# Attention outputs per query tile, and weight column sums at another place of the program

## The chip, the cores and the metric

The kernel runs on one core of a Trainium2 chip. The metric is the time of one execution on the device, in microseconds (us). A core has a matrix engine (PE, with its weight loads shown apart as PEld), a vector engine (DVE), an activation engine (ACT) and a general engine (POOL). SP issues the transfers. Each engine has a queue and executes it in order; the engines wait for one another through semaphores.

## The reference

The output of windowed attention goes through two feed-forward layers.

```
scores = q k^T / 8 - slope_h * (i - j)     for 0 <= i - j < 128, else masked
x  = softmax(scores) v                     4 batches, 8 heads of 64, 576 positions
h  = relu(x w_in1);   x2 = (s * h*h + b) w_out1      2304 tokens, 512 -> 2048 -> 512
h2 = relu(x2 w_in2);  out = (h2*h2) w_out2           512 -> 2048 -> 512
```

All values are float32.

## The kernel before

Tokens are handled in blocks of 256: two for each batch (b, u with u = 0 or 1), and one last block, the tail, of the 64 left-over positions of the four batches. The products of the feed-forward layers take each operand as a high and a low part (names ending in h and l) and make three products of them, so that 12 matmuls make one 128-row slice of the hidden layer (L338, names h) and 12 use it again (L374 in the first layer, L383 in the second, names o).

**Jobs.** One job is a call of `mlp` for one block: for each of 16 slices f, `first(f)` is 12 matmuls, a relu on ACT (L342, names r), a square on DVE (L343), and a split into high and low part (names g: a copy on ACT, L95, and a subtraction on DVE, L98, or on POOL, L101). The products with w_out of a slice follow two slices later. The jobs of the first layer are: the first halves of blocks 0 and 1 (a0, a1, 8 slices each), their other halves (c0, c1), then a2 to a6 one after the other in a loop, then a7 together with the tail, a8, which runs six slices behind it. The second layer has b0 with b1, then b2 to b6, b8, b7. `POOL_STEPS` says how many of every four slices of a job have their subtraction on POOL.

**Weights.** They arrive as 64-bit words and are converted in five operations (`convert`: ACT L120, DVE L121, ACT L122, DVE L123, POOL L124; names st), then split (names wih, wil, woh, wol with the number of the group of four slices). The weights of the first layer are converted during a0 to c0, those of the second during a7, a8 and b0.

**Attention.** `pair_unit` handles two heads (hp) of a block. `probabilities` makes the scores (L235) of two query tiles of 128, the exponentials and their sums. `outputs` scales the probabilities, transposes them in pieces of 128 x 128 (L256) into a PSUM bank t, copies the bank to pt, and multiplies by V (L265) into a bank u, where head 0 stands in the partitions 0 to 63 and head 1 in 64 to 127. A query tile has two key blocks, but the first tile of u = 0 has one. These units are hung behind the slices of the jobs before them.

**Column sums.** The b of the first layer reaches the second through the sums of w_out1 over its rows. `sum_rows` adds the high and low rows of a slice to `csum` on POOL (L488, 32 additions in all), `sum_column` adds over the partitions on PE (L511, names pc) and makes `bcol`; `load_y(i)` loads the sums of block i (xib, for blocks 0 and 1 in two parts with xjb, added at L498), scales them and adds bcol (L500, ACT), and splits them (yb0h, yb0l, ...). All of this stands in a7 and a8, as `pieces` spread over 0.9 of their steps, but `load_y(1)`, which stands behind them.

The order of each engine's queue is not that of the program: a scheduler rearranges it when the kernel is built.

Of the kernel before, what the change touches and what calls it, by code (L numbers as in the profile page):

```python
# [8 lines left out]
F32 = mybir.dt.float32  # L9
# [6 lines left out]
P = 128  # L16
# [3 lines left out]
def attention_mlp2_kernel(ctx, tc, first0, first1, qkv0, qkv1, qkvt, w_in1, w_out1, s_in, b_in, w_in2, w_out2, out):  # L20
# [20 lines left out]
    NRAW, NQKV, NPR, NPT = 3, 3, 4, 2  # L41
# [24 lines left out]
                            pattern=[[1, 2 * W]], channel_multiplier=-1)  # L66
    ones = const.tile([P, 1], F32, tag="ones", name="ones")
# [26 lines left out]
    def act_copy(o, i):  # L94
        nc.scalar.activation(o, i, AF.Copy)  # L95
# [100 lines left out]
    def pair_unit(b, u, hp):  # L196
# [48 lines left out]
        def outputs():  # L245
            raw, den, probs, pts = (made[x] for x in ("raw", "den", "probs", "pts"))
            vr = raw[:, BLK + nj * P:n].rearrange("p (j a d) -> p j a d" if early else "p (a j d) -> p j a d", j=nj, d=D)
            for a in range(2):
                tp = (psum("h", f"t{nm}").rearrange("p (i n) -> p i n", n=P) if early and not (a or u) else
                      ps.tile([P, 4, P], F32, tag="t", name=f"t{nm}{a}", bufs=1))  # L250
                m = 0
                for i, (_, ncol) in enumerate(tiles):
                    pr = probs[a][:, i, :ncol]
                    nc.vector.tensor_scalar(pr, pr, den[:, 2 * a + i:2 * a + i + 1], None, ALU.mult)
                    for j in range(ncol // P):
                        nc.tensor.transpose(tp[:, m, :], pr[:, j * P:(j + 1) * P], ident)  # L256
                        m += 1
                (nc.vector.tensor_copy if early and u <= a else act_copy)(pts[a][:, :m, :], tp[:, :m, :])
            up = ps.tile([P, 3 * P], F32, tag="u", name=f"u{nm}", bufs=1) if hp % 2 or u or not early else psum("o", f"u{nm}")

            steps = [(slice(0, 2), 0), (slice(2, 3), P)] if u == 0 else [(slice(0, 1), 0), (slice(1, 3), 0), (slice(3, 4), P)]
            steps = sorted(zip(range(nj), steps), key=lambda x: x[1][0].start - x[1][0].stop)
            for k, (j, (sl, col)) in enumerate(steps):
                for a in range(2):
                    nc.tensor.matmul(up[a * D:(a + 1) * D, col:col + (sl.stop - sl.start) * P], vr[:, j, a, :], pts[a][:, sl, :],  # L265
                                     start=(k == 0), stop=(k == nj - 1), skip_group_check=True)
            xh, xl = xt[(b, u)]
            split(xh[:, hp, :], xl[:, hp, :], up[:, :BLK], act_copy if early and u else act_mark, dve_sub)
# [143 lines left out]
    POOL_STEPS = {"a0": 4, "c1": 3, "a2": 2, "a3": 3, "a5": 3}  # L412
# [58 lines left out]
    nc.sync.dma_start(b_sb, b_in.partition_broadcast(P))  # L471
    tails = [[lambda b=b, hp=hp: tail_unit(b, hp) for hp in range(H // 2)] for b in range(B)]
    for i in range(NHALF, LAST - 1):
        more = attn(i + 2) if i + 2 < LAST and blocks[i + 2] not in xt else []
        pending += tails[i - 3] if i > 2 else []
        mlp([(f"a{i}", xt.pop(blocks[i]), finish1(f"a{i}", acc_dram[i]))], wts1, second_t, FS, pending + more[:5])
        pending = more[5:]

# [5 lines left out]

    def sum_rows(g, j):

        for w in (wts1[g][2], wts1[g][3]):
            nc.gpsimd.tensor_tensor(csum, csum, w[:, j, :].bitcast(F32), ALU.add)  # L488
# [16 lines left out]
    csum = bp.tile([P, DM], F32, tag="csum", name="csum", bufs=1)  # L505
    nc.gpsimd.memset(csum, 0.0)

# [12 lines left out]
    pieces = [lambda g=g, j=j: sum_rows(g, j) for g in range(NG) for j in range(GF)] + [lambda: None] * 6  # L520
    pieces += [sum_column, lambda: ys.update({0: load_y(0)})]
# [63 lines left out]
```

## Time and profile before

| | |
|---|---|
| median of 3 runs | 1028.07 us (1027.82 to 1029.13) |
| profiled execution | 1028.07 us, of which the span of the profile is 1026.3 us |
| mean granted TensorE clock | 0.985 of full speed |
| PE busy | 97% |
| DVE, ACT, POOL busy | 53%, 46%, 17% |

The span is what the profiler saw of the program; 1.8 us lie outside of it. A busy share is a mean over stages that have different limits.

### The profile page before, as it was taken

To read this page: it belongs to the slowest core of one execution; us is meant where nothing else is said; L and a number is where in the kernel's file an instruction comes from. 1 tells how busy PE (TensorE), PEld (TensorE's weight loads), DVE (VectorE), ACT (ScalarE), POOL (GpSimd) and SP (SyncE) were. 2 spreads that over 40 slices of the span, in tenths; PEclk is the share of its full clock that TensorE was granted. 3 is DMA by queue.
4 is the path that set the end of the run, shared out by engine and by line. 5 is a ranking of instruction groups with operands and counts; after the bars stand their busy time and mean duration, and the time that the engine had idled before them with its cause. 6 is when DMAs were issued, how large, how long until landed. Compare 5 with 4: busy or idle time off the path is not lost.

```text
span 1026.3 us, 17924 instructions
## 1 busy us (share of the span) xinstructions
PE 995.3 (97%) x7048; PEld 893.3 (87%) x7048; DVE 540.7 (53%) x1283; ACT 476.1 (46%) x1178; POOL 179.3 (17%) x156
## 2 busy tenths in 40 slices
PE   7898999999999999999899989999999999999998
PEld 4586898889889889899799979989998999999897
DVE  6989864343444534534687788775333333323232
ACT  6676554554544545544324576674232323323232
POOL 4655411001110001100694212210000000000000
PEclk9799999999999999999999999999999999999999
DMA  7264342111121211210402244422010000000000
GB/s 286 83 216 139 103 119 62 47 38 37 52 74 34 70 48 52 67 45 25 159 27 82 83 145 144 147 100 83 2 42 1 22 21 1 21 1 21 1 21 21
DMA packets 39556, 70.36 MB, mean 69 GB/s; under 512 B 4016, under 2 KB 16304, under 8 KB 39472
## 3 DMA queue, kind: packets, MB, share of 16 engines
q1 hardware_dynamic: 39472, 69.22, 20.5%
q8 instruction: 55, 0.90, 0.4%
q14 instruction: 29, 0.24, 0.1%
HBM read 58.72 MB, written 10.49 MB: 67 GB/s over the span
## 4 chain that ended last, share of the span: by engine, by line
PE 81%; DVE 11%; ACT 3%; issue 2%; DMA 2%; SPq 0%; DVEq 0%; ACTq 0%
PE ob L383 17%; PE hb L338 17%; PE ha L338 17%; PE oa L374 15%; PE u L265 4%; PE s L235 3%; DVE st L121 2%; PE hc L338 2%; PE oc L374 2%; PE t L256 2%; DVE gb L98 1%; DVE ra L343 1%; DVE ga L98 1%; DVE rb L343 1%; DVE wol L98 1%
## 5 line engine op out<-in xcount | busy, mean ns | idle before, releaser
L374 PE MATMUL oa<-ga,woh 128*128 128x256 f32 x1024 | 198.2, 288 | 8.7 <-DVE ga L98 8.1
L383 PE MATMUL ob<-woh,gb 128*128 128x512 f32 x576 | 198.5, 392 | 0.9 <-DVE gb L98 0.9
L374 PEld LDWEIGHTS oa<-ga,woh 128*128 128x128 f32 x1024 | 161.8, 192 | 14.1 <-DVE ga L98 9.2
L374 PE MATMUL oa<-ga,wol 128*128 128x256 f32 x512 | 146.2, 287 | 1.2 <-DVE wol L98 1.2
L343 DVE TENSOR_TENSOR rb<-rb 128x256 f32<-128x256 f32 x144 | 64.3, 447 | 120.3 <-ACT rb L342 117.2
L383 PEld LDWEIGHTS ob<-woh,gb 128*128 128x128 f32 x576 | 108.5, 189 | 21.0 <-DVE gb L98 1.3
L343 DVE TENSOR_TENSOR ra<-ra 128x256 f32<-128x256 f32 x128 | 76.5, 602 | 89.2 <-ACT ra L342 88.5
L342 ACT ACTIVATE rb<-hb 128x256 f32<-128x256 f32 x144 | 55.0, 383 | 136.9 <-PE hb L338 126.7
L383 PE MATMUL ob<-wol,gb 128*128 128x512 f32 x288 | 113.5, 394 | 0.0
L374 PEld LDWEIGHTS oa<-ga,wol 128*128 128x128 f32 x512 | 98.6, 193 | 3.9 <-issue 2.3
L98 DVE TENSOR_TENSOR gb<-rb,gb 128x256 fp32r<-128x256 f32 x144 | 68.6, 479 | 61.3 <-ACT gb L95 36.8
L124 POOL TENSOR_TENSOR st<-st 128x1024 int32<-128x1024 int32 (+1 forms) x34 | 65.7, 1932 | 155.0 <-DVE st L123 134.7
L95 ACT ACTIVATE gb<-rb 128x256 fp32r<-128x256 f32 x144 | 60.0, 417 | 67.4 <-DVE rb L343 67.4
L95 ACT ACTIVATE ga<-ra 128x256 fp32r<-128x256 f32 x128 | 52.8, 415 | 69.7 <-DVE ra L343 69.0
L342 ACT ACTIVATE ra<-ha 128x256 f32<-128x256 f32 x128 | 47.9, 378 | 68.5 <-PE ha L338 62.3
L101 POOL TENSOR_TENSOR ga<-ra,ga 128x256 fp32r<-128x256 f32 x40 | 32.7, 822 | 222.3 <-ACT ga L95 185.4
L98 DVE TENSOR_TENSOR ga<-ra,ga 128x256 fp32r<-128x256 f32 x88 | 54.4, 622 | 27.7 <-ACT ga L95 27.3
L383 PEld LDWEIGHTS ob<-wol,gb 128*128 128x128 f32 x288 | 54.6, 189 | 6.8
L188 ACT ACTIVATE pr<-pr,nd 128x128 f32<-128x128 f32 (+1 forms) x96 | 45.1, 472 | 21.8 <-DVE nd L184 21.8
L121 DVE SCALAR_TENSOR_TENSOR st<-st 128x1024 int32<-128x1024 int32 (+1 forms) x34 | 48.2, 1419 | 11.4 <-ACT st L120 11.4
L122 ACT ACTIVATE st<-st 128x1024 f32<-128x1024 f32 (+1 forms) x34 | 37.5, 1108 | 22.8 <-DVE st L121 22.6
L235 PE MATMUL s<-raw 64*128 64x256 f32 (+1 forms) x224 | 43.1, 401 | 4.0 <-DVE nd L184 2.5
(258 smaller groups left out, 2537.8 us busy)
## 6 DMA issues: line engine op xcount, KB each, us to landing
st<-w_in SPq DMA_DIRECT2D x16, 1024.0 KB, 5.7
st<-w_out SPq DMA_DIRECT2D x14, 1024.0 KB, 4.9
raw<-qkv SPq DMA_DIRECT2D x36, 128.0 KB, 2.8
xib<-acc SPq DMA_DIRECT2D x9, 512.0 KB, 3.4
out<-obb SPq DMA_DIRECT2D x16, 256.0 KB, 2.1
raw<-qkv SPq DMA_DIRECT2D x24, 160.0 KB, 3.0
acc<-xoa SPq DMA_DIRECT2D x14, 256.0 KB, 2.0
raw<-qkv SPq DMA_DIRECT2D x12, 192.0 KB, 2.9
```

The lines of the kernel that those rows point to most:

```text
L95: nc.scalar.activation(o, i, AF.Copy)
L98: nc.vector.tensor_tensor(o, a, b_, ALU.subtract)
L121: nc.vector.scalar_tensor_tensor(l32, h32, -2 ** 31, l32, ALU.bitwise_and, ALU.bitwise_or)
L124: nc.gpsimd.tensor_tensor(l32, h32, l32, ALU.add)
L188: nc.scalar.activation(pr, pr, AF.Exp, bias=nmx, scale=-1.0, accum_out=den)
L235: nc.tensor.matmul(sps[a][:, i, :ncol], qr[rows, i * P:(i + 1) * P], kr[rows, ka:ka + ncol], start=(i == 0), stop=True, skip_group_check=True)
L265: nc.tensor.matmul(up[a * D:(a + 1) * D, col:col + (sl.stop - sl.start) * P], vr[:, j, a, :], pts[a][:, sl, :], start=(k == 0), stop=(k == ...
L338: nc.tensor.matmul(ph, w_[:, cc, j * P:(j + 1) * P], x_[:, cc, :], start=(k == 0), stop=(k == 3 * NCC - 1))
L342: nc.scalar.activation(r, ph, AF.Relu)
L343: nc.vector.tensor_tensor(r, r, r, ALU.mult)
L374: nc.tensor.matmul(po[o // 2][:, (o % 2) * BLK:(o % 2 + 1) * BLK], w_[:, j, o * P:(o + 1) * P], g[:, gi, :], start=(start and n == 0 and o ...
L383: nc.tensor.matmul(po[t], g[:, gi, t * P:(t + 1) * P], w_[:, j, :], start=(start and n == 0), stop=(stop and n == 2))
```

## The change

The diff does three things. In `outputs`, a bank t and its copy pt now hold both heads of one query tile (before: both tiles of one head). The products with V are all of 128 columns, and go through the tiles and key blocks with head 0 and head 1 in turn; `tc.issue_after(moved.ins)` is put around them. The column sums become pieces of the jobs a2 to a5 (four slices in each), `csum` is taken from the pool of constants, NRAW (buffers for finished blocks) goes from 3 to 2, and a2, a3 and a5 have no subtraction on POOL any more. The pieces of a7 and a8 are now `sum_column` and `load_y(0)` alone.

```diff
-    NRAW, NQKV, NPR, NPT = 3, 3, 4, 2
+    NRAW, NQKV, NPR, NPT = 2, 3, 4, 2
...
+    csum = const.tile([P, DM], F32, tag="csum", name="csum")
...
-            for a in range(2):
-                tp = (psum("h", f"t{nm}").rearrange("p (i n) -> p i n", n=P) if early and not (a or u) else
-                      ps.tile([P, 4, P], F32, tag="t", name=f"t{nm}{a}", bufs=1))
+            for i, (_, ncol) in enumerate(tiles):
+                tp = (psum("h", f"t{nm}").rearrange("p (i n) -> p i n", n=P) if early and not (i or u) else
+                      ps.tile([P, 4, P], F32, tag="t", name=f"t{nm}{i}", bufs=1))
                 m = 0
-                for i, (_, ncol) in enumerate(tiles):
+                for a in range(2):
                     pr = probs[a][:, i, :ncol]
                     nc.vector.tensor_scalar(pr, pr, den[:, 2 * a + i:2 * a + i + 1], None, ALU.mult)
                     for j in range(ncol // P):
                         nc.tensor.transpose(tp[:, m, :], pr[:, j * P:(j + 1) * P], ident)
                         m += 1
-                (nc.vector.tensor_copy if early and u <= a else act_copy)(pts[a][:, :m, :], tp[:, :m, :])
+                moved = (nc.vector.tensor_copy if early and u <= i else act_copy)(pts[i][:, :m, :], tp[:, :m, :])
             up = ps.tile([P, 3 * P], F32, tag="u", name=f"u{nm}", bufs=1) if hp % 2 or u or not early else psum("o", f"u{nm}")
 
-            steps = [(slice(0, 2), 0), (slice(2, 3), P)] if u == 0 else [(slice(0, 1), 0), (slice(1, 3), 0), (slice(3, 4), P)]
-            steps = sorted(zip(range(nj), steps), key=lambda x: x[1][0].start - x[1][0].stop)
-            for k, (j, (sl, col)) in enumerate(steps):
-                for a in range(2):
-                    nc.tensor.matmul(up[a * D:(a + 1) * D, col:col + (sl.stop - sl.start) * P], vr[:, j, a, :], pts[a][:, sl, :],
-                                     start=(k == 0), stop=(k == nj - 1), skip_group_check=True)
+            with tc.issue_after(moved.ins):
+                k = 0
+                for i, (ka, ncol) in enumerate(tiles):
+                    nk = ncol // P
+                    for j in range(nk):
+                        for a in range(2):
+                            nc.tensor.matmul(up[a * D:(a + 1) * D, i * P:(i + 1) * P], vr[:, ka // P + j, a, :],
+                                             pts[i][:, a * nk + j, :], start=(k == 0), stop=(j == nk - 1),
+                                             skip_group_check=True)
+                        k += 1
...
-    POOL_STEPS = {"a0": 4, "c1": 3, "a2": 2, "a3": 3, "a5": 3}
+    POOL_STEPS = {"a0": 4, "c1": 3}
...
+    def sum_rows(g, j):
+
+        for w in (wts1[g][2], wts1[g][3]):
+            nc.gpsimd.tensor_tensor(csum, csum, w[:, j, :].bitcast(F32), ALU.add)
+
+    nc.gpsimd.memset(csum, 0.0)
+    sums = [lambda g=g, j=j: sum_rows(g, j) for g in range(NG) for j in range(GF)]
     tails = [[lambda b=b, hp=hp: tail_unit(b, hp) for hp in range(H // 2)] for b in range(B)]
     for i in range(NHALF, LAST - 1):
         more = attn(i + 2) if i + 2 < LAST and blocks[i + 2] not in xt else []
         pending += tails[i - 3] if i > 2 else []
-        mlp([(f"a{i}", xt.pop(blocks[i]), finish1(f"a{i}", acc_dram[i]))], wts1, second_t, FS, pending + more[:5])
+        mlp([(f"a{i}", xt.pop(blocks[i]), finish1(f"a{i}", acc_dram[i]))], wts1, second_t, FS, zipped((pending + more[:5], 2), (sums[:4], 1)))
         pending = more[5:]
+        del sums[:4]
...
-    csum = bp.tile([P, DM], F32, tag="csum", name="csum", bufs=1)
-    nc.gpsimd.memset(csum, 0.0)
...
-    pieces = [lambda g=g, j=j: sum_rows(g, j) for g in range(NG) for j in range(GF)] + [lambda: None] * 6
-    pieces += [sum_column, lambda: ys.update({0: load_y(0)})]
+    pieces = [sum_column, lambda: ys.update({0: load_y(0)})]
```

How the queues of the engines change is shown at three places.

PE, the outputs of block (1, 1), heads 0 and 1, behind the slices 12 and 13 of c1. `t1_1_00` and `t1_1_01` are the two banks of the unit, `pr` the probabilities by head, `pt` the copies of the banks, `u` the bank of the output. Before:

```order
L256 MATMUL t1_1_00_1727<-ident_75,pr1_1_00_1645 128x128 x4
...
L256 MATMUL t1_1_01_1735<-ident_75,pr1_1_01_1646 128x128 x4
L265 MATMUL u1_1_0_1743<-pt1_1_00_1647,raw1_1_0_1640 64x256
L338 MATMUL hc1_13_1783<-x(0, 1)l_325,wih3_1198 128x256
...
L235 MATMUL s1_1_10_1823<-raw1_1_1_1814 128x256
L265 MATMUL u1_1_0_1743<-pt1_1_01_1648,raw1_1_0_1640 64x256
L265 MATMUL u1_1_0_1743<-pt1_1_00_1647,raw1_1_0_1640 64x128
L265 MATMUL u1_1_0_1743<-pt1_1_01_1648,raw1_1_0_1640 64x128
L265 MATMUL u1_1_0_1743<-pt1_1_00_1647,raw1_1_0_1640 64x128
L265 MATMUL u1_1_0_1743<-pt1_1_01_1648,raw1_1_0_1640 64x128
```

After:

```order
L257 MATMUL t1_1_00_1752<-ident_75,pr1_1_00_1670 128x128 x2
L257 MATMUL t1_1_00_1752<-ident_75,pr1_1_01_1671 128x128 x2
...
L257 MATMUL t1_1_01_1760<-ident_75,pr1_1_00_1670 128x128 x2
L257 MATMUL t1_1_01_1760<-ident_75,pr1_1_01_1671 128x128 x2
L268 MATMUL u1_1_0_1768<-pt1_1_00_1672,raw1_1_0_1665 64x128 x4
L343 MATMUL hc1_13_1810<-x(0, 1)h_333,wil3_1220 128x256
...
L268 MATMUL u1_1_0_1768<-pt1_1_01_1673,raw1_1_0_1665 64x128 x4
L379 MATMUL oc11_1603<-gc1_11_1737,wol2_886 128x256
```

The transposes of one bank now come from both heads. Before, the products were one, and later five in a row, two of them 256 columns wide; now they are four and four, each of 128 columns. They still stand at two places of the queue, and the first four stand right behind the second bank's transposes.

POOL, early in the program, between the conversions of the weight groups 0 and 1 (st, wil, wol) and the splits of a0 (ga0). Before:

```order
L101 TENSOR_TENSOR wol0_307<-st02_304,woh0_306 128x1024
L124 TENSOR_TENSOR st10_328<-st10_328 128x1024
L101 TENSOR_TENSOR wol0_307<-st03_315,woh0_306 128x1024
L101 TENSOR_TENSOR ga0_0_355<-ra0_0_352,ga0_0_355 128x256
L101 TENSOR_TENSOR ga0_1_464<-ra0_1_461,ga0_1_464 128x256
L101 TENSOR_TENSOR wil1_331<-st10_328,wih1_330 128x4x256
L124 TENSOR_TENSOR st11_467<-st11_467 128x1024
L101 TENSOR_TENSOR ga0_2_492<-ra0_2_489,ga0_2_492 128x256
L101 TENSOR_TENSOR ga0_3_613<-ra0_3_610,ga0_3_613 128x256
L124 TENSOR_TENSOR st12_628<-st12_628 128x1024
```

After:

```order
L102 TENSOR_TENSOR wol0_316<-st02_313,woh0_315 128x1024
L480 TENSOR_TENSOR csum_90<-csum_90,woh0_315 128x512
L125 TENSOR_TENSOR st10_337<-st10_337 128x1024
L102 TENSOR_TENSOR wol0_316<-st03_324,woh0_315 128x1024
L480 TENSOR_TENSOR csum_90<-csum_90,wol0_316 128x512
L102 TENSOR_TENSOR ga0_0_364<-ra0_0_361,ga0_0_364 128x256
L102 TENSOR_TENSOR wil1_340<-st10_337,wih1_339 128x4x256
L125 TENSOR_TENSOR st11_480<-st11_480 128x1024
L102 TENSOR_TENSOR ga0_1_477<-ra0_1_474,ga0_1_477 128x256
L480 TENSOR_TENSOR csum_90<-csum_90,woh0_315 128x512
L102 TENSOR_TENSOR ga0_2_505<-ra0_2_502,ga0_2_505 128x256
L480 TENSOR_TENSOR csum_90<-csum_90,wol0_316 128x512
```

Four additions of `csum` stand here among the conversions, which had none. Nine of the 32 stand ahead of the split `wol2<-st22`, eleven more ahead of the split `wol3`, and the last twelve ahead of the split `gc1_10` of c1. Before, all 32 stood after those of a6.

DVE, the start of a7 (after) and the place near the end of a8 where the same operations stood (before). `bcol` is made of the column sum, `xib` are the loaded sums of blocks 0 and 1, `yb0` and `yb1` their splits. Before:

```order
L343 TENSOR_TENSOR ra7_15_6591<-ra7_15_6591 128x256
L512 TENSOR_SCALAR bcol_95<-pc_6609,b_sb_94 128x4
L98 TENSOR_TENSOR ga7_15_6594<-ra7_15_6591,ga7_15_6594 128x256
L88 CAST yb0h_6658<-xib0_6646 128x1024
L98 TENSOR_TENSOR yb0l_6659<-xib0_6646,yb0h_6658 128x1024
L88 CAST yb1h_6920<-xib1_6908 128x1024
L98 TENSOR_TENSOR yb1l_6921<-xib1_6908,yb1h_6920 128x1024
L98 TENSOR_TENSOR wil1_6967<-st11_6975,wih1_6966 128x4x256
```

After:

```order
L99 TENSOR_TENSOR ga6_15_5889<-ra6_15_5886,ga6_15_5889 128x256
L506 TENSOR_TENSOR xib0_6338<-xib0_6338,xjb02_6343 128x512
...
L506 TENSOR_TENSOR xib1_6972<-xib1_6972,xjb10_6974 128x512
L517 TENSOR_SCALAR bcol_96<-pc_5946,b_sb_95 128x4
L124 TENSOR_SCALAR st01_6999<-st01_6999 128x1024
L506 TENSOR_TENSOR xib1_6972<-xib1_6972,xjb12_6977 128x512
L89 CAST yb0h_6350<-xib0_6338 128x1024
L99 TENSOR_TENSOR yb0l_6351<-xib0_6338,yb0h_6350 128x1024
L348 TENSOR_TENSOR ra7_0_5965<-ra7_0_5965 128x256
L89 CAST yb1h_6984<-xib1_6972 128x1024
L348 TENSOR_TENSOR ra7_1_5984<-ra7_1_5984 128x256
L99 TENSOR_TENSOR ga7_0_5968<-ra7_0_5965,ga7_0_5968 128x256
```

The splits of blocks 0 and 1 stand now between ga6_15 and ga7_0, behind two additions that wait for loads of xjb; on ACT six of the eight scalings (L508 there) stand ahead of the relu of slice 0 of a7. On PE the column sum stands between the last products of a6 and the first of a7; it stood between slices of a8. SP's queue has the same order.

## Rows read from the trace of the kernel before

**Rows 1.** The page's first part: busy time of each engine, its share of the span, and its instructions.

```profile
PE 995.3 (97%) x7048; PEld 893.3 (87%) x7048; DVE 540.7 (53%) x1283; ACT 476.1 (46%) x1178; POOL 179.3 (17%) x156
```

**Rows 2.** Busy time of each engine in five stretches, one row for each: its limits and its length, then PE, PEld, DVE, ACT and POOL busy with the number of instructions, the granted TensorE clock, the DMA share and GB/s.

```profile
78.00:110.00 32.00, 26.44 (x168) 21.18 (x168) 30.90 (x61) 20.36 (x45) 17.17 (x10) 0.89 0.37 118
110.00:145.00 35.00, 35.00 (x278) 33.06 (x277) 28.73 (x48) 20.71 (x46) 12.18 (x8) 1.00 0.43 136
145.00:490.00 345.00, 345.00 (x2744) 309.10 (x2744) 144.98 (x567) 164.67 (x502) 30.52 (x54) 1.00 0.17 51
500.00:515.00 15.00, 10.43 (x64) 9.23 (x64) 13.50 (x12) 6.60 (x9) 12.96 (x9) 0.85 0.54 203
515.00:580.00 65.00, 65.00 (x535) 65.00 (x535) 50.24 (x54) 25.66 (x53) 35.73 (x25) 0.98 0.20 70
```

**Rows 3.** The chain of work that ended last, read for 0 to 145 us: start, length, what. Two of its pieces.

```profile
79.35 2.83 DVE st L121
...
104.00 2.59 PE oa L374 x12
```

**Rows 4.** The timeline of PE around three groups of products with V, on otherwise full stretches: start, busy time, line, operation, out<-in, shape, count. The ends overlap, so cost is read from starts. Each product of the program has two records here. The last row counts all records of the products from 110 to 490 us.

```profile
154.13 0.86 PE L265 MATMUL u<-pt,raw 128*64 128x256 f32 x6
154.92 0.39 PE L338 MATMUL hc<-x(0, 1)h,wih 128*128 128x256 f32 x1
...
187.55 0.28 PE L338 MATMUL ha<-x(1, 0)l,wih 128*128 128x256 f32 x1
187.67 0.28 PE L338 MATMUL ha<-x(1, 0)h,wil 128*128 128x256 f32 x1
187.88 1.08 PE L265 MATMUL u<-pt,raw 128*64 128x256 f32 x10
188.89 0.39 PE L338 MATMUL ha<-x(1, 0)h,wih 128*128 128x256 f32 x1
...
197.70 0.60 PE L256 MATMUL t<-ident,pr 128*128 128x128 f32 x4
198.23 0.65 PE L265 MATMUL u<-pt,raw 128*64 128x256 f32 x2
198.80 0.38 PE L338 MATMUL ha<-x(1, 0)h,wil 128*128 128x256 f32 x1
...
110.00:490.00 380.00, 35.84 (x224) 18.18 (x224) 1.00 0.20 58
```

**Rows 5.** Groups of instructions by line and form. The first three rows are from 525 to 547 us, while POOL does the column sums; the last two are of the same forms of DVE from 145 to 490 us. Columns: line, engine, operation, out<-in, shapes, count | busy us, mean ns of one | idle before it, and its releaser.

```profile
L488 POOL TENSOR_TENSOR csum<-csum,woh 128x512 f32<-128x512 f32 x8 | 10.9, 1358 | 0.6
...
L343 DVE TENSOR_TENSOR ra<-ra 128x256 f32<-128x256 f32 x8 | 12.1, 1510 | 0.0
L98 DVE TENSOR_TENSOR ga<-ra,ga 128x256 fp32r<-128x256 f32 x8 | 8.2, 1028 | 3.4 <-ACT ga L95 3.4
...
L343 DVE TENSOR_TENSOR ra<-ra 128x256 f32<-128x256 f32 x75 | 31.6, 421 | 83.5 <-ACT ra L342 82.8
L98 DVE TENSOR_TENSOR ga<-ra,ga 128x256 fp32r<-128x256 f32 x43 | 18.3, 426 | 18.7 <-ACT ga L95 18.5
```

**Rows 6.** The same view from 20 to 104 us, for POOL and for DVE.

```profile
L124 POOL TENSOR_TENSOR st<-st 128x1024 int32<-128x1024 int32 x11 | 22.2, 2025 | 28.3 <-DVE st L123 15.9 <-DVE nd L192 11.1 <-DVE nd L191 1.3
L101 POOL TENSOR_TENSOR ga<-ra,ga 128x256 fp32r<-128x256 f32 x8 | 9.0, 1146 | 10.0 <-ACT ga L95 10.0
L101 POOL TENSOR_TENSOR wil<-st,wih 128x1024 fp32r<-128x1024 f32 x3 | 7.3, 2418 | 4.9 <-DVE wih L88 4.9
L101 POOL TENSOR_TENSOR wol<-st,woh 128x1024 fp32r<-128x1024 f32 x2 | 5.5, 2744 | 0.3 <-ACT woh L95 0.3
...
L121 DVE SCALAR_TENSOR_TENSOR st<-st 128x1024 int32<-128x1024 int32 x11 | 20.0, 1816 | 1.6 <-ACT st L120 1.6
L343 DVE TENSOR_TENSOR ra<-ra 128x256 f32<-128x256 f32 x10 | 7.2, 739 | 0.0
```

**Rows 7.** POOL's timeline: the split of a weight part of the third group (a `wol` of group 2).

```profile
106.55 3.16 POOL L101 TENSOR_TENSOR wol<-st,woh 128x1024 fp32r<-128x1024 f32 x1 [2.88 <-DVE woh L88]
```

**Rows 8.** What PE waited for from 500 to 515 us, its longest (engine, line, waited for: us in total, times, longest us).

```profile
PE oa L374 <- DVE ga L98: 3.3, 2, 2.7
```

**Rows 9.** DVE's timeline around the hand-over from a8 to b0, which also shows how long the forms of L88, L98 and L121 take while POOL is idle.

```profile
592.51 0.69 DVE L88 CAST yb0h<-xib 128x1024 fp32r<-128x1024 f32 x1 [1.54 <-ACT xib L500]
593.24 1.23 DVE L98 TENSOR_TENSOR yb0l<-xib,yb0h 128x1024 fp32r<-128x1024 f32 x1
...
597.83 1.22 DVE L121 SCALAR_TENSOR_TENSOR st<-st 128x1024 int32<-128x1024 int32 x1
```

**Rows 10.** The groups of 580 to 596 us by line and form: the column sum's products on PE and the scaling on ACT.

```profile
L500 ACT ACTIVATE xib<-xib,bcol,s_sb 128x256 f32<-128x256 f32 x8 | 4.0, 586 | 0.0
L511 PE MATMUL pc<-ones,csum 128*128 128x1 f32 x8 | 0.9, 240 | 0.0
```

**Rows 11.** What PE waited for from 580 to 615 us.

```profile
PE oa L374 <- DVE ga L98: 3.0, 2, 2.2
PE ha L338 <- ACT ra L342: 2.1, 1, 2.1
```

**Rows 12.** Two pieces of the chain of work from 475 to 640 us.

```profile
494.21 4.34 DMA xjb<-half
506.31 2.29 DVE st L121
```

More of the change, by code (lines that the diff above doesn't have):

```diff
@@ L94, in act_copy @@
     def act_copy(o, i):
-        nc.scalar.activation(o, i, AF.Copy)
+        return nc.scalar.activation(o, i, AF.Copy)
     def dve_sub(o, a, b_):
@@ L483, in attention_mlp2_kernel @@
     n_g[0] = -1
-    def sum_rows(g, j):
-        for w in (wts1[g][2], wts1[g][3]):
-            nc.gpsimd.tensor_tensor(csum, csum, w[:, j, :].bitcast(F32), ALU.add)
     def load_x(nm, drams):
```

## The prediction

> **What bounds the kernel now.** I read the page first: PE is busy for 995.3 us of 1026.3 [rows 1]. That is a mean over stages, so I read busy time by stretches next [rows 2]. From 145 to 490 us PE is full while DVE is at 42%: there only PE's own work counts. From 515 to 580 us PE is full again, with DVE at 77%. PE has holes in three places. From 78 to 110 us it is busy for 26.44 of 32 us and DVE for 30.90: DVE sets the pace, which the chain shows too, where a DVE conversion of 2.83 us leads to PE's next group at 104.00 us [rows 3]. From 500 to 515 us PE is busy for 10.43 us. At the pace of the stretch behind it (535 records in 65 us, 0.1215 each) its 64 records are 7.8 us of work, so 7.2 us are lost. The third place is 580 to 615 us, where PE waits for 3.0 us on DVE and 2.1 us on ACT [rows 11]. So an edit is worth what it takes from PE in the full stretches, and what it does to DVE's queue in the three holes.
>
> **Part 1, the outputs.** PE, in full stretches. A matmul of a slice starts every 0.12 us (187.55, 187.67), so what a group of products costs is the start of the next matmul, less the start of the last one, less 0.12. Ten records cost 188.89 - 187.67 - 0.12 = 1.10 us. Six records start 0.21 us after the matmul ahead of them too, so they cost 154.92 - 154.13 + 0.09 = 0.88 us. The four records more are two products of 128 columns, one for each head; they cost 0.22 us, 0.11 for each pair: the two heads, which use different halves of the array, run side by side when they stand next to each other. The two records of one 256-column product cost, with the four transposes ahead of them, 198.80 - 197.70 = 1.10 us; less 4 x 0.11 for the transposes that is 0.66. All three fit 0.24 us for a group, 0.21 for each 256-column record (two of these in each group) and 0.11 for each pair of 128-column records: 0.24 + 0.43 = 0.67; 0.24 + 0.43 + 0.22 = 0.89; 0.24 + 0.43 + 0.44 = 1.11 [rows 4].
>
> After, the queue still has two groups for a unit, since the order put around the products holds back nothing on PE. A unit of u = 1 has four products (eight records, four pairs) in each group: 2 x (0.24 + 0.44) = 1.36 against 0.67 + 1.11 = 1.78. One of u = 0 has two products and four: (0.24 + 0.22) + (0.24 + 0.44) = 1.14 against 0.67 + 0.89 = 1.56. Each saves 0.42 us. From 110 to 490 us there are 224 records [rows 4]; 12 units of u = 1 with 12 records and 10 of u = 0 with 8 are 224. So 22 x 0.42 = **-9.2 us**. Bounds: 0 if every group costs what the six records did (0.88), and -14.5 if the second group of a unit lost its 0.24 too (22 x 0.66). I take the middle, since it is built from three rows that agree. Transposes, copies and scalings keep their number; their order in a unit hides behind the slices.
>
> **Part 2, the column sums.** The diff spreads them over a2 to a5, but POOL's queue has nine of the 32 ahead of the split that ran at 106.55 us [rows 7], eleven between there and 141 us, and twelve before 162 us. What they cost in their old place: one takes 1.36 us on POOL, and DVE operations with two SBUF inputs that took 0.42 us each take 1.51 and 1.03 us while the sums run [rows 5]. That is 8 x (1.09 + 0.60) = 13.5 us for 16 sums, 0.85 us of DVE for each. PE hides it from 515 to 580 us, but not at 500 to 515 us.
>
> In the new place DVE sets PE's pace for the first nine. There POOL's conversions and splits already stretch DVE: over 44.0 us of POOL work, 11 conversions took 20.0 us instead of 11 x 1.22, and 10 squares 7.2 instead of 4.2 [rows 6, 9]. These two lines alone lose 9.6 us, 0.22 us for each us of POOL, so 0.30 us for a sum is the low end. The whole 1.36 us is the high end. I take 0.75, near the 0.85 of the nearest row, a little less as some of the nine fall where PE is waiting for transfers or is busy: 9 x 0.75 = 6.8 us. The eleven behind them add 8.3 us to a DVE that was busy for 28.73 of 35 us [rows 2]: 37 us of work in 35. DVE catches up behind 145 us, so I count 1.2 us of the 2. Together **+8.0 us** (low 2.7, high 9 x 1.36 + 11 x 0.75 = 20.5).
>
> The Trainium skill has a rule that speaks against this part: "SBUF — State Buffer", Who interferes with whom, says that a DVE operation with two inputs in SBUF and a GpSimd operation that reads SBUF share a pair of ports, and that the one that comes second waits for the whole of the other. The rows on squares and splits agree with it [rows 5]. By it each early sum could take its full 1.36 us from DVE, and the sum would end at the high end, 1031.5 us (rival A).
>
> The 32 subtractions that go from POOL to DVE are 32 x 0.43 = 14 us on a DVE that is 42% busy in that stretch: nothing. If DVE were full there, all 14 us would show. NRAW at 2 can make the second half of a finished block wait for the first one's transfer; ACT runs these copies while PE has filled banks in hand, so I count nothing, 1.6 us at most (it can bite once, where b0 and b1 finish together).
>
> **Part 3, the start of a7.** With the sums gone, DVE's conversion of 2.29 us at 506.31 takes 1.22 [rows 9, 12], and two splits, a square and an addition of xib lose what they were stretched by: four times 1.0 to 1.1 us. That is 5.2 us by which the split that PE waited for, 3.3 us in all [rows 8], comes earlier. Against it, three operations on yb0 and yb1 stand now ahead of ga7_0 (0.69 + 1.23 + 0.69 = 2.6 us, [rows 9]), six of eight scalings (3.0 us, [rows 10]) ahead of the first relu, and both wait for xjb, one load of which took 4.34 us [rows 12]. PE can do six slices of a7, 12 x 0.12 = 1.44 us each, before it needs ga7_0. I let 1.6 us of the new work show: 5.2 - 1.6 = -3.6 us. The column sum's 0.9 us on PE [rows 10] leaves a full stretch and goes into one where PE waits: -0.8. Together **-4.4 us** (0 if the new work takes all of it; -8.0 if all the loss of 7.2 us goes).
>
> **Part 4, the end of a8.** Eight scalings (4.0 us, [rows 10]) leave ACT at 590 us, and four yb operations (3.8 us, [rows 9]) leave DVE at 592 us. PE's wait of 2.1 us was for the relu behind those scalings, and 3.0 us for splits behind that DVE work [rows 11]. I take 3.5 of the 5.1 us, since the conversions of the second layer still fill DVE there: **-3.5 us** (-1 to -6).
>
> **Sum.** Against the profiled execution's own time, which is the median too: 1028.07 - 9.2 + 8.0 - 4.4 - 3.5 = 1019.0 us.
>
> **The rivals.**
>
> A. The early sums hold DVE for their full length. For: in the old place DVE and POOL ran in turn, and the squares lost 1.09 of 1.36 us [rows 5]. Against: most DVE work at the start reads PSUM or one operand. Price +20.5 instead of +8.0: 1031.5 us. It ends on the slower side once the sums cost over 19.2 us (17.1 saved, and 2.1).
>
> B. The early sums cost next to nothing, because they fall where POOL is idle and DVE waits for something else: +2 instead of +8, 1013 us. For: POOL was idle for 28.3 us ahead of its conversions from 20 to 104 us [rows 6]. Against: it waited there for DVE itself, and DVE was full.
>
> C. yb0 and yb1 take the place of the sums at the start of a7: Part 3 gives nothing, 1023.4 us. For: three loads of xjb come one after another through one buffer. Against: six slices of cover.
>
> D. The new groups of products cost what the old ones did (0.88 us each, the first bound): 1028.2 us, no change. For: the number of groups is the same. Against: the price of four records more, 0.22 us. That the heads may run one after the other is the worse end of this case.
>
> E. The change does not do what it says. This much is seen in the order: the sums are not spread but early, and the products not joined. It is in the forecast.
>
> **Chances.** The forecast 0.46, with its own range of 1015 to 1024; B 0.18, C 0.14, D 0.08, A 0.14. A measurement of this kernel tells about 0.2% (2.1 us) from no change. Forecast, B and C are faster: 0.78; D is the same: 0.08; A slower: 0.14. The range of 1011 to 1029 us holds forecast, B, C and most of D, and leaves out A and some of the two ends of the sum.
>
> **What would show it.** Part 1: groups of eight records at 0.68 us, so 28 us for the 22 units (12 x 1.36 + 10 x 1.14) where it was 37. Part 2: two-input operations of DVE above 1 us next to sums between 45 and 135 us, PE reaching its first full stretch some 8 us later than 104 us. Part 3: PE from the last slice of a6 to the seventh of a7 without a wait over 1 us. Part 4: no wait of PE for ACT's relu at the end of a8. The prediction falls if PE's first full stretch starts 20 us later or at the same time, or if the groups keep their price.

## The result and the profile after

The changed kernel takes 1040.45 us (median; 1039.25 to 1043.21) where the kernel before takes 1028.6: a ratio of 1.012, with a 95% interval of 1.0097 to 1.0142. The forecast was 1019.0 us and faster. The profiled execution has a span of 1038.1 us, 11.8 more than before. Two executions that stand far off, one of experiment 1 (2349.75 us) and one of experiment 9 (5207.63), are left out of the figures below.

The page's first part, after, answers to [rows 1]:

```profile
PE 989.6 (95%) x7176; PEld 894.0 (86%) x7176; DVE 551.8 (53%) x1315; ACT 480.3 (46%) x1178; POOL 161.8 (16%) x124
```

PE has less work (989.6 us busy, was 995.3) and a longer span. So nearly all of the loss is waiting, and the stretches say where. Busy time by stretches, after; columns as in [rows 2]. The fourth stretch lies 9.7 us later than in [rows 2], as a6 ends that much later:

```profile
78.00:110.00 32.00, 24.25 (x179) 20.35 (x176) 31.96 (x60) 19.98 (x47) 25.16 (x14) 0.95 0.37 114
110.00:145.00 35.00, 29.99 (x228) 28.13 (x227) 33.14 (x30) 17.68 (x35) 29.24 (x17) 0.95 0.32 103
145.00:490.00 345.00, 342.26 (x2829) 310.15 (x2828) 172.39 (x609) 169.16 (x510) 29.27 (x39) 0.99 0.19 54
509.70:524.70 15.00, 12.78 (x104) 12.30 (x103) 9.06 (x12) 9.35 (x15) 3.79 (x2) 1.00 0.57 214
616.60:717.00 100.40, 92.64 (x573) 82.27 (x572) 68.76 (x97) 59.07 (x112) 15.81 (x8) 0.98 0.31 109
```

From 78 to 145 us PE is busy for 24.25 + 29.99 us, where it was 26.44 + 35.00, while POOL is busy for 25.16 + 29.24 instead of 17.17 + 12.18. At the start of a7, the hole of before, PE is busy for 12.78 of 15 us, where it was 10.43, and the clock there is 1.00, where it was 0.85. And there is a new hole, in the job of b0 and b1 (616.6 to 717.0 us): 92.64 us busy in 100.4. The same job before, in the same view:

```profile
615.20:705.20 90.00, 89.12 (x573) 80.86 (x572) 67.66 (x97) 57.55 (x111) 16.07 (x8) 1.00 0.37 125
```

573 records in both, so the same work, in 90.0 us. I read the places of the jobs from PE's timeline: the start of the first or the last matmul of L338 (L343 after) of a job, in us.

| | a1 last | c1 last | a6 last | a7 first | a8 last | b0 first | b2 first |
|---|---|---|---|---|---|---|---|
| before | 120.6 | 177.9 | 501.9 | 512.9 | 605.4 | 615.2 | 705.2 |
| after | 126.8 | 193.7 | 511.6 | 519.7 | 606.1 | 616.6 | 717.0 |
| outputs alone (experiment 1) | 120.2 | 178.5 | 493.8 | 505.2 | 598.1 | 609.4 | 698.9 |
| sums held (2) | 118.3 | 176.7 | 504.5 | 513.1 | 599.6 | 611.2 | 711.2 |
| after, staggered (6) | 127.5 | 191.8 | 509.7 | 519.8 | 606.3 | 616.1 | 709.0 |
| spread, staggered (7) | 117.4 | 175.5 | 493.7 | 503.5 | 590.7 | 601.1 | 694.2 |
| spread, staggered earlier (8) | 117.9 | 176.9 | 495.1 | 504.9 | 591.2 | 598.5 | 691.5 |

Each row is one execution. The changed kernel, experiment 4 and experiment 6 have the same start, and differ there by up to 1.0 us at a1's end (126.8, 127.8, 127.5) and 2.0 at c1's (193.7, 193.8, 191.8), so the terms below hold to a us or two.

From b2 on all kernels take the same time. Against the outputs alone, the rest of the change costs 17.8 us up to the end of a6, gives back 3.3 between a6 and a7 and 7.4 from a7 to b0, and loses 10.9 in b0 and b1: 18.0 us, where the spans differ by 18.1. Of the 17.8, 15.3 are there at c1's end. The other 2.5 come between c1 and a6, where PE is busy without a break in both kernels (317.9 and 315.3 us) with 2664 matmul records in each; no run takes them apart.

Two expected things did come. The new products, on PE's timeline of the changed kernel:

```profile
187.12 0.40 PE L379 MATMUL oc<-gc,woh 128*128 128x256 f32 x2
187.44 0.66 PE L268 MATMUL u<-pt,raw 128*64 128x128 f32 x8
188.03 0.38 PE L379 MATMUL oc<-gc,wol 128*128 128x256 f32 x1
```

Two matmuls start at 187.12 and, by the pace of 0.12, at 187.24; the next one starts at 188.03. So the group of eight records costs 188.03 - 187.24 - 0.12 = 0.67 us; the forecast had 0.68. And what PE waited for from 580 to 615 us, where [rows 11] had 5.1 us:

```profile
PE oa L379 <- ACT ga L96: 2.0, 1, 2.0
```

One thing was as forecast in kind but not in size. DVE's squares and splits from 110 to 145 us, after (by line and form, columns as in [rows 5]):

```profile
L348 DVE TENSOR_TENSOR ra<-ra 128x256 f32<-128x256 f32 x7 | 9.9, 1415 | 0.0
L99 DVE TENSOR_TENSOR ga<-ra,ga 128x256 fp32r<-128x256 f32 x7 | 6.2, 885 | 1.5 <-ACT ga L96 1.5
```

These are the 0.42 us operations of [rows 5], at 1.42 and 0.89 us. And what PE waited for in the new hole:

```profile
PE ob L388 <- DVE gb L99: 3.9, 4, 2.5
PE hb L343 <- ACT rb L347: 2.1, 1, 2.1
PE ob L388 <- ACT gb L96: 1.7, 1, 1.7
```

### The profile page after: what moved, and what is told of

It reads as the page before. It is cut to its first block, busy times and chain, and to the rows that moved or that the text cites. A ratio compares the mean times of both kernels' runs of the same rounds, so it can differ in the third digit from the quotient of the medians.

```text
span 1038.1 us, 18151 instructions
## 1 busy us (share of the span) xinstructions
PE 989.6 (95%) x7176; PEld 894.0 (86%) x7176; DVE 551.8 (53%) x1315; ACT 480.3 (46%) x1178; POOL 161.8 (16%) x124
## 4 chain that ended last, share of the span: by engine, by line
PE 76%; DVE 12%; DMA 5%; ACT 3%; issue 2%; SPq 0%; DVEq 0%; ACTq 0%
PE hb L343 17%; PE ob L388 17%; PE ha L343 15%; PE oa L379 15%; PE s L236 3%; DVE st L122 3%; PE u L268 3%; PE t L257 2%; DMA st<-w_in 2%; PE oc L379 2%; PE hc L343 1%; DMA st<-w_out 1%; ACT st L121 1%; DVE ra L348 1%; DVE st L124 1%
## 5 line engine op out<-in xcount | busy, mean ns | idle before, releaser
L348 DVE TENSOR_TENSOR rb<-rb 128x256 f32<-128x256 f32 x144 | 64.3, 448 | 126.8 <-ACT rb L347 124.2
L348 DVE TENSOR_TENSOR ra<-ra 128x256 f32<-128x256 f32 x128 | 67.3, 527 | 80.1 <-ACT ra L347 79.5
L99 DVE TENSOR_TENSOR gb<-rb,gb 128x256 fp32r<-128x256 f32 x144 | 64.4, 448 | 59.0 <-ACT gb L96 58.8
L122 DVE SCALAR_TENSOR_TENSOR st<-st 128x1024 int32<-128x1024 int32 (+1 forms) x34 | 53.1, 1560 | 15.6 <-ACT st L121 15.5
L189 ACT ACTIVATE pr<-pr,nd 128x256 f32<-128x256 f32 (+1 forms) x96 | 45.6, 475 | 31.6 <-DVE nd L185 31.4
L236 PE MATMUL s<-raw 64*128 64x256 f32 (+1 forms) x224 | 45.5, 410 | 5.9 <-DVE nd L185 3.4
L185 DVE CUSTOM_DVE_ANT_0 pr<-s,bases 128x256 f32<-128x256 f32 (+1 forms) x96 | 32.9, 387 | 29.1 <-PE s L236 29.1
```

Of the source, the lines that this page charges most:

```text
L99: nc.vector.tensor_tensor(o, a, b_, ALU.subtract)
L122: nc.vector.scalar_tensor_tensor(l32, h32, -2 ** 31, l32, ALU.bitwise_and, ALU.bitwise_or)
L189: nc.scalar.activation(pr, pr, AF.Exp, bias=nmx, scale=-1.0, accum_out=den)
L236: nc.tensor.matmul(sps[a][:, i, :ncol], qr[rows, i * P:(i + 1) * P], kr[rows, ka:ka + ncol], start=(i == 0), stop=True, skip_group_check=True)
L348: nc.vector.tensor_tensor(r, r, r, ALU.mult)
```

## The experiments

**1. The outputs alone.** The kernel before with the new `outputs`.

> Only the outputs of the change (banks per query tile, products of 128 columns with the heads in turn); the column sums and the loads of y as before. Theory 1 (the outputs save 9.2 us, the early sums cost some 19 us, and some 10 us are lost in b0 and b1): 1028.6 - 9.2 = 1019.4 us, no loss at the start, PE no later than before at the first slice of c1. Rival (the new banks also delay the start, where scores, copies and products of the first blocks lie on the path): 1025 us or more, with PE's start of c1 later than 147.4 us.

Measured: 1018.52 us (three executions, 1018.48 to 1021.82), ratio 0.9898 (0.9879 to 0.9918). That is 10.8 us less than the 1029.29 of the kernel before in the same session; the profiled execution, the slowest of the three, has a span 6.3 us shorter than before. The term of 9.2 us lies between. c1 begins at 151.6 us, 147.4 before, which was the rival's sign; but its last matmul is at 178.5 (177.9 before), so hardly anything of that delay is left at c1's end.

**2. The sums held back.**

```diff
+        subs.append(nc.gpsimd.tensor_tensor(o, a, b_, ALU.subtract).ins)   # in pool_sub
...
+        with tc.issue_after(subs[-1]):
             for w in (wts1[g][2], wts1[g][3]):
                 nc.gpsimd.tensor_tensor(csum, csum, w[:, j, :].bitcast(F32), ALU.add)
```

> The changed kernel, with each pair of additions ordered on POOL behind the last subtraction of POOL that the program has issued (those of c1), so that all 32 run after 175 us, in the full stretch of a2. Theory 1: the loss at the start goes, 1040.4 - 18.9 = 1021.5 us if the loss of 10.4 us in b0 and b1 stays, 1011 us if that loss was a consequence of the late start. Rival (not the sums but the outputs delay the start): 1036 us or more.

Measured: 1035.0 us (ratio 1.006, 1.0045 to 1.0075), where 1021.5 or 1011 were expected. The start is repaired: c1's last matmul is at 176.7 us instead of 193.7, so the early sums cost 17.1 us there. The total did not follow, for two reasons. b0 and b1 still take 100 us. And all 32 additions run in a row in a2, between 177 and 222 us, which costs some 10 us too (c1's last matmul to a3's first takes 78.5 us; with the sums spread, in experiment 7, 68.5). DVE by line and form there, from 184 to 228 us, and PE's wait from 180 to 250 us:

```profile
L257 DVE TENSOR_SCALAR pr<-pr,nd 128x256 f32<-128x256 f32 x12 | 12.1, 1058 | 0.0
L350 DVE TENSOR_TENSOR ra<-ra 128x256 f32<-128x256 f32 x8 | 8.9, 1117 | 1.1 <-ACT ra L349 1.0
```

```profile
PE oa L381 <- DVE ga L99: 5.1, 2, 3.1
```

The scalings of the probabilities (L254 before, L257 here) and the squares take over 1 us on average. DVE is busy for 34.38 of the 44 us, and PE waits for it all the same. From c1 to a6 PE's waits come to 6.4 us. At the end of the longest one (3.1 us, up to 206.8) the granted clock falls to 0.50 (1.2 GHz) until 212.8 us, which is some 3 us more, by an estimate of half of those 6.8 us. That a place has idle time on DVE does not make the additions free there. I read it so that a slice must come through relu, square and split in the time of two other slices; no run tests that by itself.

**3. The early sums alone.** The kernel before with part 2 of the change; the column sum and `load_y(0)` at their old place (38 empty pieces ahead of them).

> The kernel before with only the column sums of the change (csum among the constants, pieces of a2 to a5, NRAW 2, no subtraction on POOL in a2, a3 and a5); outputs as before, and the column sum and load_y(0) behind 38 empty pieces, so at their old place. Theory 1: +18.9 at the start, -3 at the start of a7, where the sums are gone: 1044.5 us, with b0 and b1 as long as before (90 us). Rival (the sums cost the forecast 8 us, and the outputs the rest): 1033.5 us.

Measured: 1048.09 us (ratio 1.0191, 1.0165 to 1.0216). 1044.5 us had been expected, with b0 and b1 at 90. a6 ends 20.0 us later than before, and b0 and b1 take 101.1 us, although y had not moved. The 101.1 hold 22 more matmul records than the 90.0 of before, since b0's first slice stands ahead of a part of a8's last products. A stretch with the same work in all kernels, but for the column sum's 0.9 us, is a7's first matmul to b2's first: 196.3 us here, 192.3 before, 193.7 in experiment 1, 197.2 after. By this measure too the second loss does not need the new outputs or the new place of y, but it is 4.0 us.

**4. y at its old place.**

```diff
-    pieces = [sum_column, lambda: ys.update({0: load_y(0)})]
+    pieces = [lambda: None] * 38 + [sum_column, lambda: ys.update({0: load_y(0)})]
```

> The changed kernel, with the column sum and load_y(0) behind 38 empty pieces, so at their old place at the end of a8. Theory 1a (the new place of y empties a8's end, PE comes to b0 sooner than the converted weights, and b0 and b1 give the gain back): the hole of 5 us at the end of a8 returns and b0 and b1 lose 5 us less or nothing, 1036 to 1040 us. Theory 1b (the new place of y has changed the order of the queues in b0 and b1, and that is the loss): 1040.4 - 10.4 + 5 = 1035 us with b0 and b1 at 90 us. Rival (the loss in b0 and b1 has to do with NRAW or with the sums): 1045 us, b0 and b1 still 100 us.

Measured: 1036.8 us (ratio 1.0075, 1.0057 to 1.0093), and b0 and b1 take 101.3 us (again with 22 more records in them). The total is that of theory 1a, but its reason fell: b0 and b1 did not lose less. From a7's first matmul to b2's first it takes 196.3 us, 1.0 less than in the changed kernel, and the total is 3.7 us less. So the new place of y gained nothing here. What had changed in the four kernels that lose there, and not in experiment 1? SP's timeline of the loads of w_in2 and w_out2 (a row is a round of two: the first one's issue, the time from there to the end of the second one's issue of 0.4 us), before:

```profile
607.91 7.03 SPq L155 DMA_DIRECT2D st<-w_in  x2
624.57 7.38 SPq L155 DMA_DIRECT2D st<-w_out  x2
640.37 7.29 SPq L155 DMA_DIRECT2D st<-w_in  x2
656.91 7.33 SPq L155 DMA_DIRECT2D st<-w_out  x2
```

After:

```profile
610.48 3.79 SPq L156 DMA_DIRECT2D st<-w_in  x2
628.16 3.83 SPq L156 DMA_DIRECT2D st<-w_out  x2
646.19 3.69 SPq L156 DMA_DIRECT2D st<-w_in  x2
664.62 3.79 SPq L156 DMA_DIRECT2D st<-w_out  x2
```

Before, the two loads of a round start 7 us apart, and a round takes 16.7, 15.8 and 16.5 us. After, they start 3.4 us apart, and a round takes 17.7, 18.0 and 18.4. There are two staging buffers. In step, both load and then both are converted; out of step, one loads while the other is converted. What puts them out of step is seen on ACT, before:

```profile
586.03 1.17 ACT L95 ACTIVATE wih<-st 128x1024 fp32r<-128x1024 f32 x1
...
590.42 4.03 ACT L500 ACTIVATE xib<-xib,bcol,s_sb 128x256 f32<-128x256 f32 x8
594.36 1.13 ACT L95 ACTIVATE wih<-st 128x1024 fp32r<-128x1024 f32 x1
```

After:

```profile
589.37 1.18 ACT L96 ACTIVATE wih<-st 128x1024 fp32r<-128x1024 f32 x1
...
594.02 1.14 ACT L96 ACTIVATE wih<-st 128x1024 fp32r<-128x1024 f32 x1
```

These are the copies of the two halves of group 1. Before, the eight scalings of y stand between them, and the second buffer is free 8 us after the first. In the changed kernel they are in a7; in experiments 3 and 4 they stand behind both copies, here in experiment 4, whose first copy is at 588.44 us:

```profile
593.09 1.16 ACT L96 ACTIVATE wih<-st 128x1024 fp32r<-128x1024 f32 x1
...
596.01 3.06 ACT L508 ACTIVATE xib<-xib,bcol,s_sb 128x256 f32<-128x256 f32 x6 [1.46 <-DVE bcol L517]
```

That became theory 2.

**5. Memsets in place of the additions.** Three memsets of csum, which read nothing, for each addition; the column sums are left out of this kernel.

> The changed kernel with three memsets of csum (0.52 us each, they read nothing) in place of each addition; the weight column sums are left out by this. The memsets stand among the same conversions. Theory 3 (an addition costs because DVE operations with two inputs wait while POOL reads): DVE's operations keep their short times next to memsets, the loss at the start goes, 1021.5 us, with b0 and b1 still at 100 us. Rival (the additions cost because POOL is occupied, and its conversions and subtractions come later): 1040 us.

Measured: 1034.77 us (ratio 1.0059, 1.0042 to 1.0076). Neither theory: c1's last matmul is at 187.2 us, 6.6 sooner than after, and 10.5 later than without sums. DVE from 30 to 165 us by line and form, with memsets:

```profile
L348 DVE TENSOR_TENSOR ra<-ra 128x256 f32<-128x256 f32 x16 | 9.9, 626 | 1.1 <-ACT ra L347 1.1
L124 DVE TENSOR_SCALAR st<-st 128x1024 int32<-128x1024 int32 x12 | 15.0, 1248 | 0.6 <-ACT st L123 0.6
```

and with additions (the changed kernel):

```profile
L348 DVE TENSOR_TENSOR ra<-ra 128x256 f32<-128x256 f32 x16 | 16.8, 1053 | 0.0
L124 DVE TENSOR_SCALAR st<-st 128x1024 int32<-128x1024 int32 x11 | 12.8, 1162 | 1.8 <-ACT st L123 1.8
```

and with neither of them there (the kernel of experiment 2, where the square is L350 and the shift L126):

```profile
L350 DVE TENSOR_TENSOR ra<-ra 128x256 f32<-128x256 f32 x16 | 9.2, 576 | 0.1
L126 DVE TENSOR_SCALAR st<-st 128x1024 int32<-128x1024 int32 x11 | 10.3, 940 | 1.5 <-ACT st L125 1.4
```

The squares take 1.05 us with additions, 0.63 with memsets and 0.58 with neither. The shift (L124, one input) takes 1.16, 1.25 and 0.94, so the memsets stretch it as the additions do. (It takes 0.70 in the kernel before from 600 to 680 us; the 0.94 has POOL's conversions beside it.) So a part of the cost is two-input operations that wait for POOL's reads. The rest is not taken apart by this run: memsets stretch the shift, and occupy POOL like the additions.

The Trainium skill, "SBUF — State Buffer", Who interferes with whom, says both: a DVE operation with two inputs in SBUF contends with a GpSimd operation that reads SBUF, and `tensor_scalar` can take both ports in a fast mode and then contends with any. The squares' row and the shift's row agree with it.

**6. The changed kernel, staggered.**

```diff
+            relus[f"{nm}_{f}"] = nc.scalar.activation(r, ph, AF.Relu).ins     # in first
...
+        with tc.issue_after(relus["a8_10"]) if n_conv[0] == 23 else nullcontext():
             split(hi, lo, l32.bitcast(F32), copy, sub)
```

> The changed kernel with one instruction held back: on ACT, the copy of the second half of group 1 of w_in2 (wih1<-st11) stands behind the relu of slice 10 of a8, about as far behind the copy of the first half as in the kernel before, where eight scalings stood between the two. Theory 2 (the two staging buffers of the second layer's weights must run out of step, so that one loads while the other is converted; the change has taken the eight scalings from between them, both load together, and a round of two takes 18 us instead of 16): the loads are issued 6 to 8 us apart from then on, rounds of 16 us, b0 and b1 take 90 to 92 us instead of 100, the whole 1031 us. Rival (the loss in b0 and b1 comes from elsewhere, as from NRAW at 2): 1040 us with b0 and b1 at 100 us.

Measured: 1031.85 us (ratio 1.0037, 1.0019 to 1.0056), 8.6 us less than after, by one instruction in another place. b0 and b1 take 92.9 us, with NRAW still at 2, so the rival of NRAW fell for 7.5 of the 10.9 us. SP's timeline of the loads:

```profile
609.33 7.35 SPq L158 DMA_DIRECT2D st<-w_in  x2
626.06 7.97 SPq L158 DMA_DIRECT2D st<-w_out  x2
643.27 7.32 SPq L158 DMA_DIRECT2D st<-w_in  x2
659.87 6.70 SPq L158 DMA_DIRECT2D st<-w_out  x2
```

The loads are issued 6.3 to 7.6 us apart, in rounds of 16.7, 17.2 and 16.6 us.

**7. Spread and staggered.** POOL has one subtraction of four slices in a2 to a5, and each pair of additions is ordered behind the last of these (as in experiment 2), with the edit of 6.

> The same, and the additions are really spread: a2 to a5 have one subtraction of four slices on POOL, and each pair of additions is ordered on POOL behind the last subtraction issued, so that they stand in eights by job, two to four in a row. Theory 1 with theory 2 (the early sums cost 18.9 us, b0 and b1 the rest): 1040.4 - 18.9 - 9.4 = 1012 us, if four additions in a row are hidden by slices of a2 to a5. Rival (additions cost some 0.3 us of PE each wherever a slice is used two slices after it is made, as 32 in a row in a2 cost 9.5 us): 1021 us.

Measured: 1018.65 us (ratio 0.9896, 0.9881 to 0.991). POOL's timeline in a2:

```profile
187.70 1.32 POOL L485 TENSOR_TENSOR csum<-csum,woh 128x512 f32<-128x512 f32 x1
189.10 1.36 POOL L485 TENSOR_TENSOR csum<-csum,wol 128x512 f32<-128x512 f32 x1
190.54 1.36 POOL L485 TENSOR_TENSOR csum<-csum,woh 128x512 f32<-128x512 f32 x1
191.98 1.29 POOL L485 TENSOR_TENSOR csum<-csum,wol 128x512 f32<-128x512 f32 x1
199.96 0.73 POOL L104 TENSOR_TENSOR ga<-ra,ga 128x256 fp32r<-128x256 f32 x1 [6.69 <-PE oa L383]
200.65 1.29 POOL L485 TENSOR_TENSOR csum<-csum,woh 128x512 f32<-128x512 f32 x1
202.02 1.30 POOL L485 TENSOR_TENSOR csum<-csum,wol 128x512 f32<-128x512 f32 x1
218.01 0.73 POOL L104 TENSOR_TENSOR ga<-ra,ga 128x256 fp32r<-128x256 f32 x1 [14.69 <-ACT ga L96]
```

At most four in a row now, and from c1's last matmul to a6's last it takes 318.2 us, as in the changed kernel (317.9), which has no additions there: spread, they are free to within 0.3 us. The time is 6.6 us above the 1012 expected. Of the 28.3 us to be saved, 17.9 came up to the end of a6 and 7.3 in b0 and b1; from a6 to b0 2.4 were lost again (107.3 us, 105.0 after), which no run takes apart.

**8. Staggered one round earlier.** `n_conv[0] == 19` and `relus["a8_4"]` in place of 23 and `a8_10`.

> Spread sums, and the staggering one round earlier: the copy of the second half of group 0 of w_in2 is held behind the relu of slice 4 of a8, in place of that of group 1. Theory 2: all rounds from the first are out of step, 16 us each, the last weights are ready 3 to 5 us earlier and the 3 us that b0 and b1 still lose go: 1015.5 us. Rival (what b0 and b1 still lose is no matter of the rounds): 1018.5 us.

Measured: 1012.61 us (ratio 0.9846, 0.9832 to 0.9861), the fastest of all: 1.5% below the kernel before, and 6.0 us below experiment 7, where 3 were expected. The last split of weights starts at 666.5 us, 2.8 sooner than in experiment 7. But the expected reason did not come: b0 and b1 take 93.0 us, as in experiments 6 and 7, and not 90. In the traces the gain lies between a7's first matmul and b0's first (93.7 us, 97.6 in experiment 7).

**9. The reverse: in step.** Experiment 1, with the first of the two copies ordered behind the eight scalings.

> The reverse of the staggering: the kernel with the new outputs alone, where eight scalings stand between the two copies of group 1 of w_in2 on ACT, and with the first of these copies ordered behind the scalings, so that the two copies stand side by side; all else is the same. Theory 2: both loads are issued 3.4 us apart from then on, rounds of 18 us in place of 16, b0 and b1 take 99 to 100 us in place of 89.5, the whole 1030 us. Rival (the distance of the loads does not matter): 1020 us.

Measured: 1027.64 us (ratio 0.9993, 0.9983 to 1.0003): 9.1 us more than experiment 1 by one instruction in another place, where 10 were expected. The spans of the two profiled executions differ by 4.4 us, as that of experiment 1 is its slowest. From a7's first matmul to b2's first it takes 199.4 us instead of 193.7; b0 itself begins sooner, ahead of a part of a8's last products. SP's timeline:

```profile
605.99 1.85 SPq L157 DMA_DIRECT2D st<-w_in  x2
624.59 3.80 SPq L157 DMA_DIRECT2D st<-w_out  x2
642.32 3.72 SPq L157 DMA_DIRECT2D st<-w_in  x2
659.97 3.44 SPq L157 DMA_DIRECT2D st<-w_out  x2
```

Rounds of 18.6, 17.7 and 17.7 us, the loads of a round 1.5 to 3.4 apart.

**10. Eight additions early.** Experiment 7 with the additions of group 0 left at their early places.

> The kernel with spread sums and the staggered weights, but with the eight additions of weight group 0 left at their early places among the first conversions. Theory 1 (each early addition costs about 0.7 us, the same for the first twelve of them as 8.5 us up to the end of a1 in the changed kernel): 1018.7 + 8 x 0.7 = 1024 us, all of it before 130 us. Rival (the loss comes from the additions behind 106 us only, or only from many in a row): 1019 to 1020 us.

Measured: 1022.02 us (ratio 0.9941, 0.9924 to 0.9958), 3.4 us above experiment 7, between the 1024 of theory 1 and the 1019 to 1020 of the rival. a1 ends 7.1 us later; ten more matmul records stand ahead of that point (649 instead of 639), some 1.2 us at the pace of 0.12, so an addition costs 0.7 us. c1 and a6 end 5.1 later, and b0 starts 3.2 later: a part of what the start loses is not seen at the end. That the pace of the weights' rounds hides it is likely, but not shown.

## Why the prediction was wrong, step by step

The measured time is above the forecast and above every rival; the dearest, A, had 1031.5 us.

- **Part 1** (-9.2): right, in the price of a group (0.67 us) and, within the scatter, in the sum. By the method of Part 1, all groups of products from 110 to 490 us cost 36.7 us before and 28.3 in experiment 1, and from c1's last matmul to a6's last it takes 8.6 us less there. Rival D fell.
- **Part 2** (+8.0): that the early sums stretch DVE where it sets the pace was right, the size was not: 17.1 us. The first term, nine additions at 0.75 us, was near: up to a1's end, twelve additions cost 8.5 us (126.8 against 118.3), of which ten more records ahead of that point are some 1.2, so about 0.6 each. The failed term is the second: "DVE catches up behind 145 us, so I count 1.2 us of the 2", and the last twelve additions had no term at all. The twenty additions behind a1 cost the rest, some 9 to 10 us up to the end of c1. The stretches show that DVE had no room there: it is busy for 33.14 of 35 us from 110 to 145 us, and PE waits, for more than 0.2 us the last time at 160.3 us. In the kernel before the last one ends at 104.0 [rows 3], in experiment 1 at 139.5 (0.4 us); so the sign of being wrong, 20 us later, had come. I had set DVE's work against its time in a window, while two-input operations there grew to 0.89 and 1.42 us. The price of the whole is near that of rival A, 20.5, but not by A's reason: 17.1 us over 32 additions is 0.53 each, not 1.36 for nine. And 2.5 us more between c1 and a6, where the forecast counted nothing, are open.
- **Part 3** (-4.4): the gain came, -3.3 between a6 and a7, and rival C fell. In the six other kernels with y at its new place it is 1.3 to 2.8 (8.6 to 10.1 us from a6's last matmul to a7's first, 11.4 in experiment 1). One wait of 1.4 us is left, of the column sum for a copy of ACT; the sign had been none over 1.
- **Part 4** (-3.5): not borne out as a gain. The waits that it named did shrink, from 5.1 to 2.0 us, and from a7 to b0 the changed kernel takes 7.4 us less than experiment 1, where this part and the column sum had -4.3. But in experiment 4, with both back at their old place, these waits come to 3.5 us (580 to 616 us), and b1's first matmul comes 100.5 us after a7's first, where it is 99.7 after and 107.1 in experiment 1. So 6.6 of the 7.4 us come without that move; what they come from is not shown. That the number has the forecast's sign is luck.
- **What was not in it** (+10.9): b0 and b1. The step that failed is in Part 4: I took the eight scalings off ACT's queue and priced the room that they leave, but did not ask what they had held apart. Behind them stood the copy that frees a staging buffer, so they set the distance of the loads for the rest of the second layer. Experiments 6 and 9 move that one copy in both directions, for 8.6 and 9.1 us. I had read the weights' conversion as load on ACT and DVE, not as a loop of load, conversion and release with a period of its own. Of the 10.9 us, 3.4 to 3.7 stay when the loads are out of step (92.9 to 93.2 us in experiments 6 to 8, 89.5 in experiment 1); no run takes them apart.

With 17.8 in place of 8.0, and all else as forecast, the sum would be 1028.8 us, no change; by this sum it takes the second loss to make the kernel slower. In spans of the profiled executions the terms give 1026.3 - 6.3 + 17.8 - 3.3 - 7.4 + 10.9 = 1038.0 us, where 1038.1 were measured; they are differences along one chain, so this closes by itself and proves no cause. By medians experiment 1 saves more (10.8) and the rest costs more (21.9), since its profiled execution is its slowest.

Open: how much of the early additions' cost is the ports and how much POOL's queue (experiment 5 has both). That the additions were cheap in their old place because a slice is used there four slices later, not two, was only argued; no run changed that distance.

## What to carry to other kernels

When a step leaves an engine's queue, look at what stood right behind it: if that frees a buffer, the step was also a delay, and the loop of that buffer may have lived on it. Where two staging buffers feed a loop, try putting them out of step on purpose, by one ordered instruction; here the distance had come about by accident. And work that is meant to be spread must be held in the queue: here the scheduler put additions meant for a2 to a5 among the first conversions, where the kernel was most pressed.

## What the runs showed of the hardware

With four or fewer in a row, the additions on POOL (1.3 us each) cost PE nothing that shows (318.2 us against 317.9), while 32 in a row cost 10 us in the same job, where DVE is busy for less than half of the time in the kernel before [rows 2]. A part of those 10 us is the clock, which fell to 0.50 (1.2 GHz) for 6.8 us at the end of a wait of PE of 3.1 us. Memsets on POOL, which read nothing, left a one-input shift on DVE at 1.25 us, where it takes 0.94 without them, but the two-input squares at 0.63 (0.58 without).
